# Regrouping the attention-to-feed-forward hand-over and the last products of a fused kernel

## The chip, the cores and the metric

One core of a Trainium2 chip. The metric is the device time of one execution in microseconds (us). "Span" is the length of the one profiled execution. Times inside a trace are from the start of its span. The engines: PE multiplies matrices (PEld is the row of its weight loads), DVE works on vectors, ACT does exponentials and copies, POOL and SP (SyncE) start transfers. Sums of products lie in PSUM, a memory that is divided into banks.

## The reference

Sliding-window attention (8 batches, 8 heads, 576 positions, head size 64, window 32), then an expert layer with an ELU (exp(h) - 1 below zero, h above) on the 4608 x 512 result:

```python
scores = scale * np.matmul(q, k.transpose(0, 1, 3, 2))
mask = np.abs(pos[:, None] - pos[None, :]) <= window
...                                      # softmax over the masked scores
x = attn @ v                             # -> [4608, 512]
h = x @ w_in                             # [4608, 2048]
g = np.where(h > 0.0, h, np.exp(np.minimum(h, 0.0)) - 1.0)
out = g @ w_out                          # [4608, 512], float32
```

## The kernel before

The feed-forward layer is done in 144 steps: 18 tiles of 256 tokens, each in 8 steps of 256 hidden units. A step has a first product (`mm1`, w_in: eight matmuls of 256 columns), an exponential on ACT, "minus one" and the ELU's last operation on DVE, and an output product (`mm2`, w_out: four matmuls of 512 columns). Attention is done in "pairs" of two blocks of 64 queries: scores, exponential (ACT), mask (DVE), values (`pv`, PE), normalization (DVE), transposes (PE), copy of the transposed tile (ACT). Steps 0 to 3 belong to the first token tile, which needs pairs 0 and 1; step 4 is the first of the second tile and needs pairs 2 and 3. So the rest of attention's start and the first steps are interleaved by hand with `at(step, slot, function, ...)`. `rotate_v` is a DVE copy that makes Vo, a copy of v shifted by 64 positions, which half of the value products read:

```python
    for i in (2, 3):
        at(0, "mid", rotate_v, 0, 2, VS - 1, (i - 2,))     # half of Vo
        at(0, "mid", mask, i)
        at(1, "mid", idle, (4, 2)[i - 2], "y1")            # products on zeros
        at(1, "mid", pv, i)
        at(2, "dve", normalize, i)
        at(3, "mid", x_transpose, i)
        at(3, "mid", x_evac, i, nc.scalar)
    at(1, "end", idle, 1, "y1")
...
    def x_transpose(i):                    # x_st is the weight side
        ...
        for do in range(NDO):
            nc.tensor.transpose(pt[:, do, :], x_st[:, 2 * do:2 * do + 2, :], ident)
...
    def mm2(kk, parts=(0, 1)):             # cut
        for ts in parts:
            for j in range(FG):
                nc.tensor.matmul(psY[t][ts], lhsT=g_t[kk][:, j, ts * 128:(ts + 1) * 128],
                                 rhs=w_out_sb[:, s * FG + j, :], ...)
        if last and s == STEPS - 1:        # last token tile: copy and send
            for ts in parts:
                for z in range(1 + ts):    # ts 0: whole tile; ts 1: two halves
                    ...
                    copy_on((nc.vector, nc.scalar)[z], y_sb[:, c], psY[t][ts][:, c])
                    (nc.scalar if z else nc.sync).dma_start(out_t[t, :, ts, c], y_sb[:, c])
...
    for kk in range(NSTEP + LAG):
        run(kk, "first")
        if 1 <= kk < NSTEP:
            elu(kk - 1)
        run(kk, "dve")
        if kk < NSTEP:
            mm1(kk)
        run(kk, "mid")
        for n in {2: (), 3: (0, 1), 4: (), 5: (2, 3)}.get(kk, (kk - LAG,) if kk >= LAG else ()):
            if n < NSTEP - 2:
                mm2(n)
            elif n == NSTEP - 1:
                for ts in range(2):
                    for m in (n - 1, n):
                        mm2(m, (ts,))
        run(kk, "end")
```

The softmax here doesn't subtract the row's maximum and nothing guards it: scores larger than these inputs give would overflow.

## Time and profile before

| | before |
|---|---|
| time, median of three runs (lowest, highest) | 305.61 us (305.57, 305.97) |
| span of the profiled run | 304.5 us |
| first w_in product starts | 16.17 us |
| early stretch: from there to step 4's product | 9.40 us |
| full stretch: from there to the start of the last ELU half ("last gate tile") | 273.57 us |
| end: from there to the end of the span | 5.32 us |

The four parts add to 304.46 us, the span. The first row of these four is the landing of a transfer that the change leaves alone.

Keep in mind that the records of consecutive matmuls overlap: those of 512 columns last 380 ns on average, though they start 217 ns apart in the steady part.

### The profile page before, as it was taken

The page shows a single profiled execution, that of the slowest core. Times are in us where ns is not written, and L with a number is a line of the kernel's source. Part 1 is how long each engine was busy: PE and PEld are TensorE (multiplying, and loading weights), DVE is VectorE, ACT ScalarE, POOL GpSimd, SP SyncE. Part 2 cuts the span into 40 slices and gives each one's busy share as a digit, 9 for nine tenths or more (in the row PEclk, how much of TensorE's full clock was granted, in tenths as well). Part 3 has the DMA queues.
Part 4 walks back from the last instruction along what each step waited for, and adds up shares of the span by engine and source line. Part 5 has one row for each costly group of instructions (what it writes and reads, how often), then busy time and mean ns, then how long its engine had stood idle before and what let it go on. Part 6 is the DMA issues. An engine that isn't in the chain of part 4 may idle for free.

```text
span 304.5 us, 7644 instructions
## 1 busy us (share of the span) xinstructions
PE 296.0 (97%) x3091; PEld 197.4 (65%) x3091; DVE 242.2 (80%) x473; ACT 168.6 (55%) x254; POOL 48.6 (16%) x68
## 2 busy tenths in 40 slices
PE   8789999999999999999999999999999999999995
PEld 3456666677676666666666666666667666666662
DVE  6867688978888887988798879887988787877664
ACT  3654556778664567546754675467535353534331
POOL 8836100910003100230013001400000000000000
PEclk9999999999999999999999999999999999999999
DMA  9999999998755997999799969996921111111011
GB/s 191 177 201 205 183 272 413 295 168 182 177 176 158 297 126 187 246 319 157 164 251 303 196 157 268 325 159 116 281 57 71 34 71 34 72 37 69 2 69 70
DMA packets 92117, 52.81 MB, mean 173 GB/s; under 512 B 76594, under 2 KB 81970, under 8 KB 92082
## 3 DMA queue, kind: packets, MB, share of 16 engines
q1 hardware_dynamic: 47330, 35.61, 43.3%
q0 software_dynamic: 42880, 10.10, 40.9%
q10 hardware_dynamic: 1872, 6.62, 5.8%
q8 instruction: 24, 0.39, 0.6%
q14 instruction: 11, 0.09, 0.1%
HBM read 36.70 MB, written 15.34 MB: 171 GB/s over the span
## 4 chain that ended last, share of the span: by engine, by line
PE 90%; DMA 3%; DVE 2%; POOL 2%; ACT 1%; issue 1%; DVEq 0%; POOLq 0%; ACTq 0%
PE ps L602 41%; PE psY L640 40%; PE psS L336 4%; PE psS L304 3%; DMA w_in_sb<-in_moe_w_in_dram 3%; PE ptx L279 1%; POOL Ve L142 1%; POOL c L136 1%; PE psXT L357 1%; DVE g_sb L626 1%; ACT pu L315 1%; DVE pm L324 0%; DVE m_sb L615 0%; PE ptx L274 0%; ACT e_sb L609 0%
## 5 line engine op out<-in xcount | busy, mean ns | idle before, releaser
L609 ACT ACTIVATE e_sb<-ps 128x512 f32<-128x512 f32 (+1 forms) x145 | 86.3, 595 | 120.6 <-PE ps L602 113.0
L602 PE MATMUL ps<-xT,w_in_sb 128*128 128x256 bf16 x1152 | 149.2, 273 | 1.4 <-DMA w_in_sb<-in_moe_w_in_dram 1.4
L640 PE MATMUL psY<-w_out_sb,g_sb 128*128 128x512 bf16 x576 | 147.6, 380 | 0.2 <-DVE g_sb L626 0.2
L602 PEld LDWEIGHTS <-w_in_sb 128*128 128x128 bf16 x1152 | 110.6, 98 | 39.7 <-DMA w_in_sb<-in_moe_w_in_dram 1.9
L626 DVE SCALAR_TENSOR_TENSOR g_sb<-ps,m_sb 128x512 bf16<-128x512 f32 (+1 forms) x145 | 99.4, 686 | 12.6
L615 DVE TENSOR_SCALAR m_sb<-e_sb 128x512 bf16<-128x512 f32 x144 | 62.5, 434 | 38.3 <-ACT e_sb L609 36.5
L640 PEld LDWEIGHTS <-g_sb 128*128 128x128 bf16 x576 | 54.5, 98 | 39.0 <-DVE g_sb L626 0.6
L142 POOL DMA_DIRECT2D Ve<-in_v_dram x40 | 35.4, 897 | 139.7 <-PE psS L336 79.9
L315 ACT ACTIVATE pu<-psS 128x1024 bf16<-128x1024 f32 x36 | 36.5, 1021 | 1.4 <-PE psS L304 1.4
L348 DVE TENSOR_TENSOR x_st<-psS,rc 128x512 bf16<-128x512 f32 x36 | 24.9, 692 | 1.2
L324 DVE TENSOR_TENSOR pm<-pu,masks 128x1024 bf16<-128x1024 bf16 x36 | 24.6, 683 | 0.6 <-ACT pu L315 0.5
L234 ACT CAST qkb<-f 128x768 bf16<-128x768 f32 (+1 forms) x29 | 25.0, 860 | 0.0
L336 PEld LDWEIGHTS <-pm 128*64 128x64 bf16 x576 | 11.2, 111 | 9.9 <-DVE pm L324 8.7
L336 PE MATMUL psS<-Ve,pm 128*64 128x65 bf16 x320 | 13.6, 197 | 0.9 <-DVE pm L324 0.9
L236 DVE COPY y_sb<-psY 128x512 f32<-128x512 f32 (+1 forms) x19 | 12.7, 671 | 1.0 <-PE psY L640 1.0
L304 PEld LDWEIGHTS <-kT 64*128 64x128 bf16 x576 | 9.5, 95 | 4.9 <-issue 4.0
L336 PE MATMUL psS<-Vo,pm 128*64 128x65 bf16 x256 | 12.0, 196 | 0.2 <-DVE Vo L153 0.2
L304 PE MATMUL psS<-qT,kT 64*128 64x64 bf16 x576 | 11.8, 191 | 0.5 <-DVE kT L236 0.5
L234 ACT COPY y_sb<-psY 128x512 f32<-128x512 f32 (+1 forms) x18 | 10.3, 571 | 3.0 <-DVE y_sb L236 3.0
L153 DVE COPY Vo<-Ve 64x1040 bf16<-64x1040 bf16 x24 | 10.3, 431 | 1.5 <-DMA Ve<-in_v_dram 0.8
L395 PE MATMUL ps_idle<-zeros 128*128 128x512 bf16 x27 | 9.5, 482 | 1.3 <-DVE zeros L194 1.3
L234 ACT COPY qT<-ptx 128x1152 bf16<-128x1152 bf16 (+2 forms) x8 | 7.5, 971 | 3.9 <-PE ptx L279 3.0
(36 smaller groups left out, 72.4 us busy)
## 6 DMA issues: line engine op xcount, KB each, us to landing
out_dram<-y_sb SPq DMA_DIRECT2D x35, 256.0 KB, 3.5
f<-in_q_dram SPq DMA_DIRECT2D x12, 576.0 KB, 5.6
f<-in_k_dram SPq DMA_DIRECT2D x12, 576.0 KB, 7.9
in_dram<-qkb ACTq DMA_DIRECT2D x10, 576.0 KB, 3.9
Ve<-in_v_dram POOLq DMA_DIRECT2D x24, 128.0 KB, 11.0
w_in_sb<-in_moe_w_in_dram POOLq DMA_DIRECT2D x4, 512.0 KB, 9.9
w_out_sb<-in_moe_w_out_dram POOLq DMA_DIRECT2D x4, 512.0 KB, 12.8
Ve<-in_v_dram POOLq DMA_DIRECT2D x16, 96.0 KB, 10.5
```

The lines of the kernel that those rows point to most:

```text
L142: nc.gpsimd.dma_start(out=V_e[b % 3][p0:p1, m, :, 0:D], in_=v[b, :, lo + p0:lo + p1, :].rearrange("h p d -> p h d"))
L234: nc.scalar.copy(d_, s_)
L304: nc.tensor.matmul(psS[:, h % 2, hp * 128 + z * QB:hp * 128 + (z + 1) * QB], lhsT=kT[b % 2][base:base + 64, KPAD + hp * S + QB * qb - WIN: ...
L315: nc.scalar.activation(pu, _bap(psS, [psS.ap[0], [1, 1024]]), AX.Exp, scale=SCALE)
L324: nc.vector.tensor_mul(pm, pu, _bap(mm, [mm.ap[0], [0, H], [1, 2 * QB]]))
L336: nc.tensor.matmul(psS[QB * z:QB * (z + 1), par, hp * VD:(hp + 1) * VD], lhsT=pm[:, par * HP + hp, z * QB:(z + 1) * QB], rhs=vv[:, qb // 2 ...
L348: nc.vector.tensor_mul(x_st, _bap(psS, [psS.ap[0], [VD, HP], [512, 2], [1, D]]), _bap(rc, [rc.ap[0], [2, HP], [1, 2], [0, D]]))
L602: nc.tensor.matmul(ps[:, j, :], lhsT=w_in_sb[:, do, fo * 128:(fo + 1) * 128], rhs=xT[t][:, :, do, :], start=(do == 0), stop=(do == NDO - 1))
L609: nc.scalar.activation(e_sb, ps, AX.Exp)
L615: nc.vector.tensor_scalar(m_sb, e_sb, -1.0, None, ALU.add)
L626: nc.vector.scalar_tensor_tensor(g_t[kk][:, z * w:(z + 1) * w, :], ps, 0.0, m_t[kk][z], ALU.max, ALU.min)
L640: nc.tensor.matmul(psY[t][ts], lhsT=g_t[kk][:, j, ts * 128:(ts + 1) * 128], rhs=w_out_sb[:, s * FG + j, :], start=(s == 0 and j == 0), sto ...
```

## The change

The intent is to start step 2's product earlier: its way is barred by step 0's ELU, which reads the buffer of sums that step 2 will write and which DVE does only after pair 3's mask. So the ELU goes ahead of the mask, pair 3's values go behind step 2's product, the zero product between them is dropped, pair 3's transposes go between the first two output products, and the subtraction of step 2 goes from DVE to ACT (step 1's was there already). In the last two steps, one matmul (second half tile, step 142, j = 0) goes ahead of the wait for the last gate tile.

```diff
+    at(0, "mid", rotate_v, 0, 2, VS - 1, (0,))
+    at(0, "mid", mask, 2)
+    at(0, "mid", rotate_v, 0, 2, VS - 1, (1,))
+    at(1, "dve", mask, 3)                     # behind step 0's ELU
+
+    at(1, "mid", idle, 4, "y1")
+    at(1, "mid", pv, 2)
+    at(1, "mid", idle, 2, "y1")
+    at(2, "dve", normalize, 2)
+    at(2, "mid", pv, 3)                       # behind step 2's product
+    at(2, "mid", normalize, 3)
     for i in (2, 3):
-        ...                                   # the lines shown above
         at(3, "mid", x_transpose, i)
         at(3, "mid", x_evac, i, nc.scalar)
-    at(1, "end", idle, 1, "y1")
+        at(3, "mid", lambda n: mm2(n), i - 2)
...
-            if kk == 1:
+            if kk in (1, 2):
                 nc.scalar.activation(m_sb, e_sb, AX.Copy, bias=-1.0)
...                                            # mm2 now takes (ts, j) parts
-        for n in {2: (), 3: (0, 1), 4: (), 5: (2, 3)}.get(
+        for n in {2: (), 3: (), 4: (), 5: (2, 3)}.get(
...
-                for ts in range(2):
-                    for m in (n - 1, n):
-                        mm2(m, (ts,))
+                mm2(n - 1, ((0, 0), (0, 1), (1, 0)))
+                mm2(n, ((0, 0), (0, 1)))
+                mm2(n - 1, ((1, 1),))
+                mm2(n, ((1, 0), (1, 1)))
```

More of the change, by code (lines that the diff above doesn't have):

```diff
@@ L488 @@
         at(0, "mid", exponential, i)
-    for i in (2, 3):
-        at(0, "mid", rotate_v, 0, 2, VS - 1, (i - 2,))
-        at(0, "mid", mask, i)
-        at(1, "mid", idle, (4, 2)[i - 2], "y1")
-        at(1, "mid", pv, i)
-        at(2, "dve", normalize, i)
+    at(0, "mid", rotate_v, 0, 2, VS - 1, (0,))
[8 more added lines that the diff above has]
+    at(2, "mid", normalize, 3)
+    for i in (2, 3):
         at(3, "mid", x_transpose, i)
         at(3, "mid", x_evac, i, nc.scalar)
-    at(1, "end", idle, 1, "y1")
+        at(3, "mid", lambda n: mm2(n), i - 2)
     at(4, "dve", swap_pools)
@@ L630, with mm2 @@
     out_t = out.rearrange("(t ts p) c -> t p ts c", p=128, ts=TT // 128)
-    def mm2(kk, parts=(0, 1)):
+    def mm2(kk, parts=((0, 0), (0, 1), (1, 0), (1, 1))):
         t, s = order[kk]
@@ L637, in mm2 @@
         last = t == NT - 1 and s == STEPS - 1
-        for ts in parts:
-            for j in range(FG):
-                nc.tensor.matmul(
-                    psY[t][ts],
-                    lhsT=g_t[kk][:, j, ts * 128:(ts + 1) * 128],
-                    rhs=w_out_sb[:, s * FG + j, :],
-                    start=(s == 0 and j == 0),
-                    stop=(s == STEPS - 1 and j == FG - 1))
+        for ts, j in parts:
+            nc.tensor.matmul(
+                psY[t][ts],
+                lhsT=g_t[kk][:, j, ts * 128:(ts + 1) * 128],
+                rhs=w_out_sb[:, s * FG + j, :],
+                start=(s == 0 and j == 0),
+                stop=(s == STEPS - 1 and j == FG - 1))
         if last and s == STEPS - 1:
-            for ts in parts:
+            for ts in sorted({ts for ts, _ in parts}):
                 for z in range(1 + ts):
```

## The prediction

> **What bounds the kernel now.** I first cut the span into stretches (busy time by stretch: length, then PE, weight loads, DVE, ACT and POOL, the granted clock, DMA share, GB/s) to see where PE, the engine with 97% of the span, has any gap to give.
>
> ```profile
> 20.00:25.60 5.60, 5.60 (x67) 3.69 (x67) 5.32 (x11) 2.96 (x6) 1.61 (x2) 1.00 1.23 206
> 25.60:100.00 74.40, 74.18 (x826) 50.61 (x825) 59.22 (x115) 47.86 (x68) 18.02 (x21) 1.00 1.26 224
> 100.00:297.70 197.70, 197.70 (x1992) 133.54 (x1990) 161.87 (x313) 106.20 (x165) 13.64 (x16) 1.00 0.75 155
> ```
>
> From 25.6 us to 297.7 us PE is busy for 271.88 of 272.10 us, and the list of waits from 25.5 to 290 us names none of a matmul. Nothing inside that stretch can be gained by this change; it can only be made to begin earlier or be followed by a shorter end. Before 16.17 us PE waits for the first quarter of w_in (a transfer of 8.41 us that stands in the chain), which the change does not touch. So all of it must come from 16.17 to 25.6 us or from the last 7 us.
>
> In the early stretch I read the chain of waits and then the timeline (start, duration, engine, line, what, count). The chain runs through ACT's two exponentials, the mask of pair 2 and the second half of Vo, and turns to PE at 20.00. From there on it is PE alone:
>
> ```profile
> 20.42 0.54 PE ps_idle L395 x2
> 20.96 0.38 PE psS L336 x16
> 21.34 0.32 PE ps_idle L395
> ```
>
> The timeline of the same stretch gives the two engines whose order changes:
>
> ```profile
> 19.52 0.42 DVE L153 COPY Vo<-Ve 64x1040 bf16<-64x1040 bf16 x1
> ...
> 19.98 0.69 DVE L324 TENSOR_TENSOR pm<-pu,masks 128x1024 bf16<-128x1024 bf16 x1
> ...
> 20.35 0.60 PE L395 MATMUL ps_idle<-zeros 128*128 128x512 bf16 x2
> ...
> 20.59 1.28 DVE L626 SCALAR_TENSOR_TENSOR g_sb<-ps,m_sb 128x512 bf16<-128x512 f32 x2
> ...
> 21.27 0.39 PE L395 MATMUL ps_idle<-zeros 128*128 128x512 bf16 x1
> ...
> 21.50 1.91 PE L602 MATMUL ps<-xT,w_in_sb 128*128 128x256 bf16 x16
> ...
> 22.02 0.69 DVE L348 TENSOR_TENSOR x_st<-psS,rc 128x512 bf16<-128x512 f32 x1
> ...
> 22.86 0.69 DVE L348 TENSOR_TENSOR x_st<-psS,rc 128x512 bf16<-128x512 f32 x1
> ...
> 23.24 0.76 PE L357 MATMUL psXT<-ident,x_st 128*128 128x128 bf16 x8
> ...
> 23.84 1.89 PE L640 MATMUL psY<-w_out_sb,g_sb 128*128 128x512 bf16 x8
> 23.94 1.07 ACT L234 COPY xT<-psXT 128x512 bf16<-128x512 bf16 x2
> ...
> 25.57 0.60 PE L602 MATMUL ps<-xT,w_in_sb 128*128 128x256 bf16 x4
> ```
>
> The reader is to see that PE has no idle note after 20.00: it is full, but part of what fills it is work on zeros (ps_idle), two such products at 20.35 and one at 21.27, which only bridge the time until DVE has delivered. The second step's ELU result (20.59, two of them) comes after pair 3's mask, so the third product of the feed-forward layer (21.50) begins late. The last stretch:
>
> ```profile
> 297.79 1.67 PE L640 MATMUL psY<-w_out_sb,g_sb 128*128 128x512 bf16 x7
> ...
> 299.62 1.25 PE L640 MATMUL psY<-w_out_sb,g_sb 128*128 128x512 bf16 x5 [0.16 <-DVE g_sb L626]
> 300.05 0.69 DVE L236 COPY y_sb<-psY 128x512 f32<-128x512 f32 x1 [0.48 <-PE psY L640]
> ...
> 300.91 0.42 DVE L236 COPY y_sb<-psY 128x256 f32<-128x256 f32 x1 [0.17 <-PE psY L640]
> 301.37 0.37 ACT L234 COPY y_sb<-psY 128x256 f32<-128x256 f32 x1 [3.00 <-DVE y_sb L236]
> ```
>
> Here PE has seven products to do while DVE makes the last gate tile, then stands until 299.62, then has five left. The last two copies follow one another.
>
> **What the skill says.** "TensorE: Matmul & The Clock Gate", section "Back-to-back issue gap", gives columns over 2.4 GHz plus 2.5 ns for one product, so about 216 ns for 512 columns, and below that a pipelined rate of 131 ns. The trace agrees with the first and not the second: in the steady end phase one step of eight products of 256 columns and four of 512 takes 1.735 us (steps at 284.76, 286.50 and 288.23), 4096 columns, hence 0.217 us for 512. The profile's mean of 380 ns for such a product includes its drain and is no cost. "PSUM — Partial Sum Buffer", section "PSUM bank collisions raise a hardware error", says that ACT and DVE must not read one bank and partition quadrant at the same time; the trace agrees in that ACT's copy at 301.37 was released by DVE's copy of the other half of the same tile, which ended at 301.33. So that tail is serial after the change too. "ScalarE: Activation LUTs", section "Rules for kernel authors", says to put an add on VectorE because it is faster there; the trace agrees, 0.63 us for the subtraction on ACT (one at step 1 already) against 0.42 us on DVE, so the move pays only if ACT has the time.
>
> **The change, part by part.** The compiled order shows on PE: the third product moves ahead of pair 3's values, the zero product between them goes, and pair 3's transposes go between the two output products that follow. On DVE: step 0's ELU goes ahead of pair 3's mask; one subtraction leaves. On ACT: that subtraction is added. (The diff says two subtractions on ACT, but step 1's was there; only step 2's is new.) POOL and SP keep their order.
>
> (1) DVE. From 19.94 to 21.9 us it does three operations of some 0.64 us spacing in another order: ELU 0, mask 3, ELU 1 rather than mask 3, ELU 0, ELU 1. Their sum is the same, so the normalizations should stay at 21.79 and 22.63. ELU 0 should end near 20.62, mask 3 near 21.3, ELU 1 near 21.9.
>
> (2) PE. The hand-over from DVE to PE costs 0.06 us (Vo ended at 19.94, its product started at 20.00). Two zero products from 20.35 end at about 20.35 + 0.45 = 20.80 to 20.89; ELU 0 is there at 20.68, so step 2's product starts at some 20.85, without a wait. It takes 8 x 0.109 = 0.87 us, to 21.72; mask 3 is there at 21.36. Pair 3's values take 0.38 us (the chain), to 22.10; ELU 1 is there at 21.96, so step 3's product runs to 22.97. Pair 2's normalized tile is ready at 22.71 + 0.06 = 22.77. Four transposes take half of 0.60 us (from 23.24 to 23.84 there are eight), to 23.27, then 4 x 0.217 = 0.87 us to 24.14, four transposes to 24.44, then 0.87 us to 25.31. Before, that point was 25.57. What is gone is one zero product: 21.50 - 21.27 = 0.23 us. No other work left PE. That is the gain: 0.23 us, though the product moves up by some 0.65 us, for the work it passes is only done later.
>
> (3) ACT. The exponential of step 2 ended 1.67 us after its product started (21.50 to 23.17), so it will end near 22.52; the added subtraction ends near 23.15, when step 3's exponential can start (1.07 us after 22.10, 23.17). So it lies in idle time (ACT idles 1.73 us before its exponential at 22.57). DVE loses 0.42 us from the queue at 23.47, off the path.
>
> (4) The end. Of twelve products in the last two steps and the one before, one goes ahead of the wait: eight before, four after 299.62. The eight fit: six of them end at 297.79 + 6 x 0.217 = 299.09, the two others by 299.53. After the wait PE ends 0.217 us earlier. But DVE copies the first half tile from 300.05 to 300.74 and only then can copy the second, which it began at 300.91. It can start at about 300.77: the gain is 0.14 us, the rest becomes a wait for DVE. Copy, ACT's copy and the last transfer follow in the same spacing.
>
> Sum: 0.23 + 0.14 = 0.37 us of 305.61, 0.12%: 305.24 us.
>
> **The rivals.** Rival 1, a wait takes the place of the zero product. Step 4's product needs pair 3's transposed tile from ACT. Its transposes now start at 24.14; before, a lone block of transposes took 0.43 us until ACT's copy started (13.76 to 14.19), the copy 0.58: ready at about 25.2, against 25.31 when PE wants it. A slack of 0.1 us is thin. The first output weights are the other: POOL issued them at 11.72, they landed 11.1 us later, 22.82, and the moved product wants them at 23.27 (0.45 us to spare); the second quarter of w_in landed at 10.97 + 9.3 = 20.27 against 20.85. If either fails by some tenths, the start gives 0 to 0.1 us and the total is 305.4 to 305.5.
>
> Rival 2, the order pays more. Were PE held back by DVE throughout this stretch, the ELU's earlier place (0.65 us) and the subtraction (0.42 us) would both come through, and the time would be 304.6 to 304.8. Against it: PE shows no idle time from 20.00, and the sum of its work there does not change except for one zero product.
>
> Rival 3, the gain is given back later, at something that comes at a fixed time. The third quarter of w_in landed 12.2 us after 18.62, 30.8, and is wanted at 33.2; nothing in the stretch to 297.7 shows a matmul waiting for a transfer. This would leave 0.14 us: 305.47. Another way to lose: the transposes, split into two blocks, take more switching time; I have 0.05 us for that at most, as an estimate from the 0.1 us by which two zero products ahead of pair 3's values (0.54 us) exceed 2 x 0.217.
>
> **Range and chances.** The three runs before lie within 0.40 us, as wide as the gain. So the predicted time is 305.25 us, 304.8 at the low end (rival 2 in part, or a luckier landing of w_in) and 305.75 at the high end (no gain, noise upward). 2% would be 6.1 us; the two stretches that can change are together only some 16 us long, mostly of work that stays. Faster 0.01, within 0.98, slower 0.01.
>
> **What would show it.** Right: in the timeline after, step 2's product starts at about 20.85 and the long full stretch (step 4's product) at about 25.3; normalizations at 21.8 and 22.6; one zero product fewer (26); in the end four products after the last gate tile, and the full tile's copy followed at once by the half's; the span 304.1 to 304.2. Wrong: an idle note on PE between 20.8 and 25.4, above all at step 4's product released by ACT's copy of the transposes; a DVE row moved later; or the second copy still waiting for PE. The number itself fails if w_in's first quarter lands at another time than 16.1 us, for then everything shifts with it.

## More of the kernel before

The page's line of busy times, whose last figure for each engine is its number of records:

```profile
PE 296.0 (97%) x3091; PEld 197.4 (65%) x3091; DVE 242.2 (80%) x473; ACT 168.6 (55%) x254; POOL 48.6 (16%) x68
```

PE and its weight loads (PEld) have as many records each, so nothing is missing from this trace.

## The result, and the profile after

Timed side by side, five runs each: before 305.57 us (305.34 to 305.97), after 305.14 us (304.82 to 305.83). The ratio is 0.999, interval 0.9975 to 1.0005. The interval doesn't exclude no gain at all. Six more runs of the changed kernel (e10) gave 0.9981 (0.9962 to 1.0000). Differences of some tenths of a microsecond can't be settled by timing in this case; all verdicts below rest on intervals within traces.

The page's busy line after:

```profile
PE 291.2 (96%) x3037; PEld 197.0 (65%) x3090; DVE 241.6 (80%) x472; ACT 169.7 (56%) x255; POOL 48.6 (16%) x68
```

PEld has one record fewer than before, the zero product. DVE has one fewer and ACT one more, the subtraction. That PE's busy time fell by 4.8 us is no gain: 53 matmul records are missing from this trace (3037 against 3090 weight loads).

The span went from 304.46 to 303.40 us. That is 1.06 us, and only a third of it belongs to the change:

| | before | after | difference |
|---|---|---|---|
| first w_in product starts | 16.17 | 15.42 | 0.75 |
| early stretch | 9.40 | 9.03 | 0.37 |
| full stretch | 273.57 | 273.58 | -0.01 |
| end | 5.32 | 5.37 | -0.05 |

The first row is luck. The transfer of the first quarter of w_in took 7.63 us here and 8.41 us before. In the eleven experiments below, the product that waits for it started anywhere between 14.85 and 15.72 us, although the programs don't differ up to there. The profiled execution of the kernel before (16.17) was the latest of all; it took 306.17 us, 0.56 more than the median of 305.61 us. So every comparison is made from that product's start on. The early stretch in the timeline after (start, duration, engine, line, what, count; a note in brackets is the engine's idle time before and what ended it):

```profile
15.42 1.05 PE L607 MATMUL ps<-xT,w_in_sb 128*128 128x256 bf16 x8 [0.59 <-DMA w_in_sb<-in_moe_w_in_dram]
...
19.23 0.69 DVE L631 SCALAR_TENSOR_TENSOR g_sb<-ps,m_sb 128x512 bf16<-128x512 f32 x1
...
19.84 0.68 DVE L324 TENSOR_TENSOR pm<-pu,masks 128x1024 bf16<-128x1024 bf16 x1
20.05 1.04 PE L607 MATMUL ps<-xT,w_in_sb 128*128 128x256 bf16 x8
...
21.39 1.05 PE L607 MATMUL ps<-xT,w_in_sb 128*128 128x256 bf16 x8
...
22.28 0.39 PE L357 MATMUL psXT<-ident,x_st 128*128 128x128 bf16 x4
22.50 1.03 PE L644 MATMUL psY<-w_out_sb,g_sb 128*128 128x512 bf16 x3
...
23.37 0.39 PE L357 MATMUL psXT<-ident,x_st 128*128 128x128 bf16 x4
23.59 1.03 PE L644 MATMUL psY<-w_out_sb,g_sb 128*128 128x512 bf16 x4
...
24.45 1.91 PE L607 MATMUL ps<-xT,w_in_sb 128*128 128x256 bf16 x16
```

The ELU of step 0 (19.23) now stands before the mask (19.84), and step 2's product follows at 20.05. The transposes are two blocks of four, each 0.22 us from its start to the start of what follows (22.28 to 22.50, 23.37 to 23.59). Where four products show as x3, a record is missing. The end in the timeline after (PEld are weight loads; SPq and ACTq issue transfers):

```profile
298.03 0.42 DVE L631 SCALAR_TENSOR_TENSOR g_sb<-ps,m_sb 128x256 bf16<-128x256 f32 x1
298.51 0.55 PEld L644 LDWEIGHTS <-g_sb 128*128 128x128 bf16 x4 [0.43 <-DVE g_sb L631]
298.94 1.07 DVE L236 COPY y_sb<-psY 128x512 f32<-128x512 f32 x2 [0.48 <-PE psY L644]
299.66 0.81 SPq L661 DMA_DIRECT2D out_dram<-y_sb  x2
300.04 0.37 ACT L234 COPY y_sb<-psY 128x256 f32<-128x256 f32 x1 [2.78 <-DVE y_sb L236]
300.45 0.36 ACTq L661 DMA_DIRECT2D out_dram<-y_sb  x1
```

Four loads now follow the last gate tile (five before), and DVE's two copies run together without a gap. ACT's copy starts 2.01 us after the last gate tile's start, against 2.23 before (301.37 - 299.14). And yet the span ends 5.37 us after it, against 5.32. The DMA view says why. It is cut into slices of 0.1 us from 1.36 us after the last gate tile's start, each digit the busy tenths of the 16 DMA engines; first before, then after:

```profile
DMA  0000000000099999999999999610300000000000
```

```profile
DMA  0000000000099999999999999713000000000000
```

Each zero run at the left is eleven slices long. In both the last 512 KB of output go as one block without a gap, starting 2.46 us and ending 4.05 us after the last gate tile's start. The copies moved; the block didn't.

### The profile page after: what moved, and what is told of

Read it like the earlier page. It is cut to its first block, busy times and chain, and to the rows that moved or that the text cites. A ratio compares the mean times of both kernels' runs of the same rounds, so it can differ in the third digit from the quotient of the medians.

```text
span 303.4 us, 7587 instructions
## 1 busy us (share of the span) xinstructions
PE 291.2 (96%) x3037; PEld 197.0 (65%) x3090; DVE 241.6 (80%) x472; ACT 169.7 (56%) x255; POOL 48.6 (16%) x68
## 4 chain that ended last, share of the span: by engine, by line
PE 89%; DMA 3%; POOL 2%; DVE 2%; issue 2%; ACT 1%; POOLq 0%; DVEq 0%; ACTq 0%
PE ps L607 41%; PE psY L644 40%; PE psS L336 4%; PE psS L304 3%; DMA w_in_sb<-in_moe_w_in_dram 3%; PE ptx L279 1%; POOL Ve L142 1%; POOL c L136 1%; PE psXT L357 1%; ACT pu L315 1%; DVE pm L324 0%; DVE g_sb L631 0%; PE ptx L274 0%; DVE Vo L153 0%; DVE x_st L348 0%
## 5 line engine op out<-in xcount | busy, mean ns | idle before, releaser
L644 PE MATMUL psY<-w_out_sb,g_sb 128*128 128x512 bf16 x526 | 139.4, 379 | 3.1 <-issue 0.8
L620 DVE TENSOR_SCALAR m_sb<-e_sb 128x512 bf16<-128x512 f32 (+1 forms) x143 | 61.9, 433 | 37.7 <-ACT e_sb L614 35.8
L395 PE MATMUL ps_idle<-zeros 128*128 128x512 bf16 x23 | 7.8, 450 | 1.4 <-DVE zeros L194 1.3
```

The lines of the kernel that those rows point to most:

```text
L620: nc.vector.tensor_scalar(m_sb, e_sb, -1.0, None, ALU.add)
```

## The experiments

All gave correct results, all ran on one chip, and all were less than 2% apart, though the interval of e6 lies wholly above 1. The kernel before had medians of 305.47 to 305.57 us beside them. The table gives the time, and from each trace, one execution per kernel, the lengths that the argument uses:

| run | median us | ratio (interval) | first product at | step 2's product after | early stretch |
|---|---|---|---|---|---|
| before | 305.57 | | 16.17 | 5.33 | 9.40 |
| after | 305.14 | 0.9990 (0.9975 to 1.0005) | 15.42 | 4.63 | 9.03 |
| e1 | 305.48 | 0.9995 (0.9978 to 1.0012) | 15.72 | 5.15 | 9.39 |
| e2 | 305.45 | 1.0002 (0.9978 to 1.0026) | 14.85 | 5.40 | 9.62 |
| e3 | 305.35 | 0.9995 (0.9980 to 1.0010) | 15.57 | 5.22 | 9.13 |
| e4 | 305.33 | 0.9991 (0.9976 to 1.0006) | 15.24 | 4.62 | 9.39 |
| e5 | 305.47 | 1.0005 (0.9985 to 1.0024) | 15.42 | 4.71 | 9.18 |
| e6 | 306.07 | 1.0017 (1.0002 to 1.0032) | 15.57 | 4.97 | 9.44 |
| e7 | 305.43 | 1.0002 (0.9984 to 1.0020) | 15.06 | 5.15 | 9.55 |
| e8 | 305.01 | 0.9990 (0.9971 to 1.0009) | 15.33 | 4.62 | 9.03 |
| e9 | 305.69 | 1.0004 (0.9982 to 1.0027) | 14.87 | 4.76 | 9.16 |
| e10 | 304.94 | 0.9981 (0.9962 to 1.0000) | 15.20 | 4.76 | 9.22 |
| e11 | 305.54 | 1.0000 (0.9978 to 1.0023) | 15.46 | 5.32 | 9.39 |

The full stretch was 273.54 to 273.60 us in every one, so nothing gained early is given back in between.

### The early stretch: what the dropped zero product is worth

e1, the kernel before without the zero product:

```diff
-    at(1, "end", idle, 1, "y1")
```

> The kernel before without the single zero product behind pair 3's values; nothing else. Read from the trace: the stretch from the start of the first w_in product to the start of step 4's product (before 25.57 - 16.17 = 9.40 us, after 24.45 - 15.42 = 9.03). My prediction's account (PE was full, the 0.23 us are this product) expects 9.17. The new theory expects 9.40, no gain: pair 3's transposes have to wait for its normalized tile (ends 23.55, transposes at 23.61 in the kernel before), wherever the products ahead of them end.

Measured: step 2's product came 0.18 us earlier (5.15 after 5.33), and the early stretch stayed at 9.39 us. The prediction's account, in which this product alone is the gain, fell. The reason stands in a row that the prediction didn't read, the weight loads. Before, around the transposes:

```profile
23.14 0.32 PEld L357 LDWEIGHTS <-x_st 128*128 128x128 bf16 x4
23.61 0.23 PEld L357 LDWEIGHTS <-x_st 128*128 128x128 bf16 x4 [0.15 <-DVE x_st L348]
```

The same in e1:

```profile
23.15 0.23 PEld L357 LDWEIGHTS <-x_st 128*128 128x128 bf16 x4 [0.32 <-DVE x_st L348]
```

Pair 3's transposes load its normalized tile as weights, and DVE finishes that tile at 23.55. So before, PE lost 0.15 us between the fourth and the fifth transpose. PE's own row doesn't show it: each transpose's record lasts 0.22 us though they otherwise start 0.06 us apart, so the fourth one's record covers the gap, and the eight are one row of 0.76 us. In e1 the same wait is 0.32 us: the 0.18 us gained ran into it.

e2 instead splits the transposes and keeps the zero product:

```diff
         at(3, "mid", x_evac, i, nc.scalar)
+        at(3, "mid", lambda n: mm2(n), i - 2)
...
-        for n in {2: (), 3: (0, 1), 4: (), 5: (2, 3)}.get(
+        for n in {2: (), 3: (), 4: (), 5: (2, 3)}.get(
```

> The kernel before with pair 3's transposes between the two output products of steps 0 and 1, the zero product kept, DVE's order as before. The prediction's account gives the split no gain: 9.40 (or 9.45). The new theory, a hidden wait of 0.15 us of pair 3's transposes for the normalized tile, expects 9.25.

Measured: 9.62 us, longer than before's. Here the first w_in product started earliest of all (14.85), and then the moved output product had to wait for its weights. From e2's chain of work that ended last (start, duration, what):

```profile
11.81 10.67 DMA w_out_sb<-in_moe_w_out_dram
22.48 0.04 issue
22.53 1.02 PE psY L641 x4
```

That wait is 0.32 us. Besides, DVE's first copy of Vo took 0.51 us instead of 0.43, and what followed came 0.07 us later. Less both, 9.23 us remain, a gain of 0.17 over 9.40, about the hidden wait of 0.15. So e2 is a miss as it stands and agrees only after the correction. e3 does both edits:

> The two edits together, with step 0's ELU still behind pair 3's mask, pair 3's values still ahead of step 2 and step 2's subtraction still on DVE. New theory: 9.03 to 9.10, the whole early gain of the change without its three named parts. A rival, that the ELU's earlier place and the moved product carry the gain, expects 9.25 to 9.40.

Measured: 9.13 us, 0.03 above the theory's range, of which 0.07 is again a slower Vo copy (here the second, 0.49 us instead of 0.42). The second block of transposes loads its weights without a wait:

```profile
23.40 0.43 PEld L357 LDWEIGHTS <-x_st 128*128 128x128 bf16 x4
```

The gain is 0.27 (with the correction 0.34) of the change's 0.37 us, without the ELU's new place, without pair 3's values moved and without the subtraction on ACT. So the dropped product pays only where the transposes are split; the split alone gives about the hidden wait, by e2 as corrected.

e4 is the cross-check, the changed kernel with the transposes joined again:

```diff
-        at(3, "mid", lambda n: mm2(n), i - 2)
...
-        for n in {2: (), 3: (), 4: (), 5: (2, 3)}.get(
+        for n in {2: (), 3: (0, 1), 4: (), 5: (2, 3)}.get(
```

> The changed kernel with both pairs' transposes together again ahead of the two output products; all else of the change kept. New theory: pair 3's transposes wait for the normalized tile (ready 0.36 us after pair 2's have begun to be followed), so the stretch is 9.39 to 9.42 and the early gain is gone; the end stays as in the changed kernel (last gate tile's start to ACT's last copy 2.01 us against 2.23). The prediction's account expects 9.03 to 9.10 still.

Measured: step 2's product is as early as in the changed kernel (4.62), yet the early stretch is 9.39 us, so the whole early gain is gone. The loads of e4 and its transposes say where:

```profile
22.67 0.23 PEld L357 LDWEIGHTS <-x_st 128*128 128x128 bf16 x4 [0.36 <-DVE x_st L348]
22.67 0.40 PE L357 MATMUL psXT<-ident,x_st 128*128 128x128 bf16 x4 [0.19 <-DVE x_st L348]
```

The wait of 0.36 us, of which PE's own row shows 0.19, is the difference of 9.39 and 9.03. It is the same bound each time: in before, e1 and e4 DVE finishes pair 3's tile 7.38 us after the first product, the fifth transpose starts at 7.43 or 7.44, and step 4's product follows at 9.39 or 9.40, however early step 2's product was. In the changed kernel the tile comes at 7.38 too, but PE has the first output product to do until 7.95. This settles the early stretch, apart from the landing of transfers (e10).

### The early stretch: the ELU's place and the subtraction

e7 is the changed kernel with pair 3's mask ahead of step 0's ELU, as before:

```diff
-    at(1, "dve", mask, 3)
+    at(0, "mid", mask, 3)
```

> The changed kernel with pair 3's mask again ahead of step 0's ELU on DVE; PE's order as changed. Step 2's product then waits for ELU 0 (ends 0.6 us later than in the changed kernel): the stretch from the first w_in product to step 4's product becomes 9.45 to 9.60 us against 9.03 (before 9.40). If the ELU's place did not matter at all it stays at 9.03 to 9.10.

Measured: 9.55 us, 0.52 worse than the changed kernel and worse than the kernel before. Its timeline:

```profile
20.21 1.03 PE L607 MATMUL ps<-xT,w_in_sb 128*128 128x256 bf16 x8 [0.37 <-DVE g_sb L631]
```

Step 2's product, now first in PE's order, waits 0.37 us for the ELU. So the ELU's place is needed once PE's order is changed, but e3 shows that nearly the same gain comes with neither.

e8 is the changed kernel with step 2's subtraction on DVE again:

```diff
-            if kk in (1, 2):
+            if kk == 1:
```

> The changed kernel with step 2's subtraction back on DVE. Theory: it lies off the path; the stretch stays at 9.03 to 9.10 us and PE shows no wait for a gate tile. Rival, that DVE's lighter load carries part of the gain: 9.2 to 9.45.

Measured: 9.03 us, the same as the changed kernel. The subtraction's move is worth nothing here. DVE does finish pair 3's tile 0.33 us later (7.71 us after the first product, not 7.38), but the split leaves that room: the second block of transposes loads its weights at 7.77, and step 4's product isn't late.

e10 is the changed kernel again, unaltered:

> The changed kernel once more, to stand beside e9 on one chip and to show the spread of the first w_in transfer: early stretch 9.03 us if the first output weights do not land later than 7.1 us after the first product, else longer by the difference; end 5.37 us; time 0.999 of the kernel before.

Measured: median 304.94 us of six, and an early stretch of 9.22 us instead of 9.03. From its timeline:

```profile
19.95 0.77 PEld L607 LDWEIGHTS <-w_in_sb 128*128 128x128 bf16 x8 [0.47 <-DMA w_in_sb<-in_moe_w_in_dram]
```

Step 2's product, 4.76 us after the first, waited for the second quarter of w_in, which it didn't in the first trace (4.63). The other 0.06 us fit the transfer that e10's expectation had named: the first output weights landed at 7.24, and the output product that would have followed the transposes at 7.22 started at 7.28. This is the prediction's rival 1 in its second and third form, real in some executions: the earlier products stand close to the landing of these transfers. In e6 it cost most; from e6's chain:

```profile
10.72 9.78 DMA w_in_sb<-in_moe_w_in_dram
20.50 0.05 issue
20.54 1.05 PE ps L607 x8
```

There step 2's product was 0.34 us late (4.97). The whole stretch was 9.44 us, no shorter than before. So the gain of the early stretch is 0.37 us when the transfers fall well. Six traces have the changed kernel's early program: after and e8 9.03, e9 9.16 (a Vo copy took 0.55 us), e5 9.18, e10 9.22 and e6 9.44. Their mean is 9.18, a gain of 0.22 us over 9.40.

### The end

e11 is the kernel before with the end's new order alone (the last four `mm2` lines of the diff above):

> The kernel before with the last step's product moved ahead and nothing else. Prediction's account: the span ends 0.14 to 0.22 us sooner after the last gate tile (5.10 to 5.18 instead of 5.32). Theory of the end: ACT's last copy comes at 2.01 instead of 2.23 us, the block of transfers is the same from 2.46 to 4.05 us, the span ends at 5.31 to 5.38 us: no gain. Early stretch 9.40 us.

Measured: the same end as in the changed kernel within 0.02, 5.39 us after the last gate tile's start (0.01 above the theory's range). The end in all runs that tell something, in us from that start (a semaphore is the counter by which a transfer tells that it has landed; SyncE waits for all of them, one after another, before it closes, and the fifth row is when it passed the last):

| | before | after | e11 | e5 | e6 | e9 |
|---|---|---|---|---|---|---|
| first of the last transfers issued | 1.63 | 1.63 | 1.63 | 1.62 | 1.25 | 1.31 |
| ACT's last copy starts | 2.23 | 2.01 | 2.01 | 1.56 | 2.02 | 1.57 |
| output block starts | 2.46 | 2.46 | 2.46 | 2.45 | 2.08 | 2.14 |
| output block ends | 4.05 | 4.05 | 4.05 | 4.11 | 4.18 | 4.52 |
| last semaphore passed | 4.41 | 4.46 | 4.48 | 4.61 | 5.04 | 5.05 |
| span ends | 5.32 | 5.37 | 5.39 | 5.53 | 5.95 | 5.96 |

e1, e2 and e3, which keep the old end, have 5.31 to 5.33 us; e4, e7, e8 and e10, with the new one, 5.38. From the last semaphore to the end of the span it is 0.91 or 0.92 us in all six. So the new order costs some 0.05 us: SyncE passes the semaphores in a fixed order, some 0.06 us each, and the last two transfers have changed places in it. ACT's, the last to land (4.38 after, 4.39 before), is now passed ahead of the other, which leaves one more to pass.

e5 tests whether the copy sets the end. The sums of the second half tile's two halves lie in banks of their own, so ACT need not wait for DVE:

```diff
+            if t == NT - 1:
+                psY[t].append(ps_tile([128, 256], FP32, "u", "psZ"))
...                                # each product of ts == 1 in two of 256 columns
-                    copy_on(eng, y_sb[:, c], psY[t][ts][:, c])
+                    copy_on(eng, y_sb[:, c], psY[t][2] if z else psY[t][ts][:, c])
```

> The changed kernel with the last half tile's sums in two PSUM banks, so that ACT's copy of its second half waits for PE and not for DVE's copy. Measured from the last gate tile's start (298.03 in the changed kernel): ACT's copy at 2.01 us there, should come at about 1.57 us. Theory of the end: the last 512 KB are transferred without a gap from some 1.1 us after the first of them is issued, and that issue (1.63 us) does not move; so the end of the span stays at 5.35 to 5.40 us (before 5.36, after 5.37). The prediction's account (the last transfer follows the last copy in a fixed spacing) expects 4.9 to 5.0 us.

(In that text the 1.1 us from issue to block should be 0.83, and the end before 5.32.) Measured: ACT's copy 0.45 us earlier (1.56 after 2.01), the block at the same place within 0.06, the end 0.16 us later, above the range of either account. The last copy isn't what sets the end. Of the 0.16 us, 0.15 lie before the last semaphore; why it came later I have not settled.

e6 does that to the first half tile instead, so that the first transfer starts earlier:

```diff
-                for z in range(1 + ts):
+                for z in range(2):
...                                # each product of ts == 0 in two of 256 columns
+                    copy_on(eng, y_sb[:, c], psY[t][2] if z > ts
+                            else psY[t][ts][:, c])
```

> The changed kernel with the first of the two last half tiles in two banks, copied by DVE and ACT at once (some 0.42 us rather than 0.69) and written by two transfers; the last copy stays serial. Theory of the end: the first transfer is issued some 0.25 us earlier (1.36 us after the last gate tile's start), the block of transfers starts that much earlier, and the span ends at about 5.1 us instead of 5.37. Rival, that the last copy sets the end: ACT's last copy stays near 1.95 to 2.01 us and the end at 5.3 to 5.4.

Measured: the first transfer 0.38 us earlier and the block's start too (2.08 after 2.46), but its end at 4.18. It has more and smaller packets (577 in all, many of 1024 bytes, against 433). And the last transfer's semaphore stands ahead of seven others in SyncE's order: it was passed at 4.61, and the others only after it, one after another, until 5.04. The end was 0.58 us later, as was the last semaphore (5.04 after 4.46).

e9 avoids both: each half tile in two banks, copied by DVE and ACT side by side, sent in one transfer:

```diff
+                nc.vector.tensor_copy(y_sb[:, 0:256], psY[t][ts][:, 0:256])
+                nc.scalar.copy(y_sb[:, 256:512], psY[t][2 + ts])
+                nc.sync.dma_start(out_t[t, :, ts, :], y_sb)
...                                # in place of the loop over z; two more banks
```

> The changed kernel with both last half tiles in two banks each, each copied by DVE and ACT at once and sent by one transfer of 256 KB in rows of 2 KB. Theory of the end (a gapless block of transfers that begins 0.83 us after the first issue, then SyncE's waits and the closing barrier): first issue at about 1.32 us after the last gate tile's start (1.63 in the changed kernel), block from 2.15 to 3.75 us (2.46 to 4.05), span end at 4.95 to 5.05 us (5.37). Rival, that something other than these transfers sets the closing (a fixed time after PE's last product): 5.3 to 5.4. The early stretch stays at 9.03 us, so the time should be some 0.35 us under that of the changed kernel on the same chip.

Measured: the block began 0.32 us earlier, following the first transfer, but the span ended at 5.96, not near 5. The same slices of the DMA view in e9, and what they moved:

```profile
DMA  0000000289999999999987001100010000000000
GB/s 0 0 0 0 0 0 0 82 348 348 389 348 389 430 348 348 348 369 389 389 328 287 21 0 41 20 0 20 20 41 20 0 0 0 0 0 0 0 0 0
```

By +3.65 us, 31 of the 32 packets of 4 bytes that signal completion were in; then a trickle of 20 to 40 GB/s ran on for 0.9 us. The packet records don't name the engine, but they read like one DMA engine that fell behind: an instruction packet of 8192 bytes ran from +3.46 to +3.77, and eight output packets followed one by one from there to +4.51. In before and after the instruction packet ran from +4.23 to +4.73 and from +4.09 to +4.65, after the block. e6's trace shows the like, an instruction packet from +2.94 to +3.46 and late small packets one by one to +4.17. That the fetch held them up is argued from this order, not tested. So it is shown that the block's start follows the first transfer, and that neither the last copy nor the last issue sets the block's end. It is not shown that an earlier start shortens the end, since both attempts met something else. What decides when the instructions are fetched stays open. No version beat both kernels beyond the noise.

## Why the prediction was right, point by point

The time was right: 305.25 us predicted, 305.14 measured. That it agrees to 0.11 us is luck, as five runs of the changed kernel spread over 1.01 us. The sum of 0.37 us was nearly right too (0.32 in the trace: 0.37 early, -0.05 at the end), but this is luck as well: the early term was 0.14 us too small and the end's 0.19 too large, and in the second trace of the same kernel (e10) the early gain was only 0.18.

The expected span of 304.1 to 304.2 us was 303.40. Had the first w_in quarter let its product start at 16.17 as before, it would be 304.15; the prediction named this condition. It also said that the number itself would fail then; it didn't, having been reckoned from the median of the timed runs and not from the profiled one.

Step 1, DVE only permutes: right. Normalizations were expected 5.62 and 6.46 us after the first product (21.79 and 22.63 less 16.17) and came at exactly these (reciprocals at 21.04 and 21.88, less 15.42).

Step 2, PE: the order and most of the points were right. Counted from the first product:

| | predicted | measured |
|---|---|---|
| step 2's product | 4.68 | 4.63 |
| step 3's product | 5.93 | 5.97 |
| first transposes | 6.80 | 6.86 |
| first output product | 7.10 | 7.08 |
| second transposes | 7.97 | 7.95 |
| second output product | 8.27 | 8.17 |
| step 4's product | 9.14 | 9.03 |

The step that failed is "Four transposes take half of 0.60 us": the 0.60 us held 0.15 us of waiting, and four take 0.22. With it fails "What is gone is one zero product": what is gone is that product and the hidden wait, 0.37 us together instead of 0.23. And the premise "From there on it is PE alone" was wrong: it was read from a PE row that can't show this wait. By e1 the dropped product alone gives nothing, and by e4 nothing is gained without the split of the transposes.

Step 3, ACT: right. The exponential of step 2 ended at 6.30 us (6.35 predicted). The subtraction cost nothing on ACT, and by e8 it gave nothing either.

Step 4, the end: the copies came out right in kind. ACT's copy moved by 0.22 us, not 0.14: DVE's second copy started 0.65 us after its first, while the first one's record of 0.69 us was still running, and the prediction had it start 0.03 us after the record's end. But "Copy, ACT's copy and the last transfer follow in the same spacing" failed. The last transfer's data lie behind the first transfer's, which didn't move, in one block of 1.59 us. The term of 0.14 us measured -0.05.

Rivals. Rival 1 is real in part: pair 3's transposed tile was ready at 8.96 us against 9.03 wanted, so it held by 0.07; the second w_in quarter was late by 0.13 us in e10 and 0.34 in e6, and the first output weights by 0.32 us in e2 and some 0.05 in e5, e6 and e10. In e6's trace the early gain was gone, as this rival said. Rival 2 (0.65 and 0.42 us coming through) is refuted by e3 and e8. Rival 3 is refuted as written, since the full stretch is the same in all runs; but the idea was right for the end, where a transfer that doesn't move took the gain.

## What to carry to other kernels

Before counting a filler as a gain, ask what binds when it is gone, and look for waits in the row of weight loads as well as of matmuls: a full matmul row can hide them. At the end of a kernel, look for what starts the last unbroken block of output; here, moving products and copies that come after that gained nothing. When a change is smaller than the spread of the first transfer's landing, compare intervals from one event in the trace to another, not spans.

## What the Trainium skill lacked or had wrong

- "TensorE: Matmul & The Clock Gate", section "Back-to-back issue gap": its pipelined 131 ns for 512 columns wasn't seen; the steady rate is 217 ns (4096 columns in 1.735 us), as its formula for a single product says.
- The same page, "Part 4: PE-mode transpose", gives about 275 ns as the duration of one 128 x 128 bf16 transpose in a kernel. Here one record lasted 0.22 us. It lacks what such transposes cost in a row: they started 56 ns apart, and a block of four took 0.22 us to the next product's start.
- "Perfetto Trace Analysis", section "Identifying the Most-Contended Engine", warns that matmul busy time is a poor measure, because pipelined instructions look smaller. It lacks that the row can also hide a wait: of the waits of 0.15 us before, 0.32 in e1 and 0.36 in e4 in the weight loads' row, the records of PE's own row leave 0, 0.15 and 0.19.
- "Runtime: NRT & Kernel Launch", section "Instruction fetch mechanics", has the sequencer fetch through its own DMA queue, at a cost mostly hidden. No page has what a fetch can cost where it falls among the last output packets: in e9 an 8192-byte packet of 0.31 us was followed by eight output packets one by one to +4.51, where all the rest was in by +3.65 (that it held them up is argued).
- The runtime's own postamble is broken down in the pages, but none has the cost of the program's close inside the span: SyncE passes the transfers' semaphores at some 0.06 us each in a fixed order (0.43 us when seven stood behind the last to complete, e6), and 0.91 us follow in each of six traces.
